# A fused attention and MLP kernel: in-order emission against a list-scheduled program with batch 0 in halves

## The chip, the cores and the metric

One Trainium2 chip (trn2), one core of it. The metric is the device time of one execution in microseconds (us).

Engine names in the profile: PE is TensorE's matmuls, PEld its weight loads, DVE is VectorE, ACT ScalarE, POOL GpSimd, SP the queue from which most transfers are issued.

## The reference

```python
# q, k, v: (4 batches, 4 heads, 1088 tokens, 32) float32; S1, S2: (8, 32)
def phi(x):                                  # 64 features a token and head
    a = einsum('rd,bhsd->bhsr', S1, x)
    b = einsum('rd,bhsd->bhsr', S2, x)
    return einsum('bhsi,bhsj->bhsij', a, b).reshape(*x.shape[:-1], 64)
q_p, k_p = phi(q), phi(k)
kv  = einsum('bhsf,bhsd->bhfd', k_p, v)
z   = sum(k_p, axis=2)
num = einsum('bhsf,bhfd->bhsd', q_p, kv)
den = einsum('bhsf,bhf->bhs', q_p, z)[..., None] + 1e-06
x   = (num / den)                            # tokens x 128: the four heads side by side
h   = x @ w_in                               # 128 -> 2048
g   = maximum(h, 0) + alpha * minimum(h, 0)
out = g @ w_out                              # 2048 -> 128, float32
```

Both kernels rewrite the last part: with W = w_in · diag(alpha) · w_out, the output is x @ W + relu(x @ w_in) @ ((1 - alpha) w_out). So a group of 512 tokens needs 16 hidden products, 16 output products and one product with W, all in bf16. The attention part stays in fp32.

## The kernel before

Keys and queries are loaded in pieces of 32 floats, one transfer for each head:

```python
def load_main(t, src, b):
    for h in range(H):
        nc.sync.dma_start(t[:, :, h], AP(src, offset=(b*H + h)*S*D,
                          ap=[[NJ*D, 128], [D, NJ], [1, D]]))
```

A half batch of queries (512 tokens) is transposed on TensorE, so that the four heads' 32 channels lie on 128 partitions; the features are made for pairs of heads, 64 rows by 128 columns; numerator and denominator for pairs of heads too:

```python
def feat(S_):                        # called for Sa and for Sb
    ps = psum.tile([128, 2, 512], F32, tag="w2")
    for p in range(2):
        nc.tensor.matmul(ps[:, p, :n], S_[64*p:64*(p+1)],      # 64 rows, 128 columns
                         s["qT"][64*p:64*(p+1), :n])
# ... and in nd():
for o in (1, 0):                     # denominator, numerator
    for p in range(2):
        nc.tensor.matmul(ps[64*p:64*(p+1), o], kvz[b][:, p, 64*o:64*(o+1)],
                         s["qp"][:, p])                          # 128 rows, 64 columns
```

The MLP keeps its output features-by-tokens, so each group's output is copied, transposed on TensorE and copied again. The order of work is that of the Python program, in which streams of steps are merged by rough weights:

```python
run(rest_steps(0, "t"))
run(merge(k_steps(0, "t", "h"), setup_steps("h")))      # keys of batch 0, weights
run(merge(k_steps(1, "t"), q_main(0, 0, "h") + q_main(0, 1, "h")))
for b in range(B):                                       # MLP of b beside the keys of b+2
    ...                                                  # and the queries of b+1
    run(merge(m_, ks, qs))
```

## Time and profile before

| | before |
|---|---|
| time, median of 5 | 184.43 us (183.06 to 189.14) |
| span of the profiled run | 179.3 us, granted clock 0.997 |
| first MLP matmul | 55.5 us |
| TensorE busy | 150.5 us, 84% of the span |
| VectorE, ScalarE busy | 83.7, 79.6 us |

The page gives busy times by engine and, in rows of 40 digits, the busy tenths of each slice of the span. The prediction below shows the lines that matter. How to read them: a full row for one engine and half-full rows for the others point to that engine, but "busy" on TensorE is drawn from records that overlap (a record of 0.38 us follows its predecessor by 0.215 us). So the starts of successive records are what a matmul costs.

### The profile page before, as it was taken

How to read it: one execution, taken by the hardware profiler on the slowest of the kernel's cores; microseconds unless marked ns; L12 is line 12 of the kernel's file. 1: busy time of each engine (PE TensorE's matmuls, PEld its weight loads, DVE VectorE, ACT ScalarE, POOL GpSimd, SP SyncE). 2: the span in 40 equal slices, each digit the busy share in tenths (PEclk: the TensorE clock that was granted, in tenths of full speed). 3: DMA queues.
4: the chain of work that ended last, by engine and by line, in shares of the span. 5: the costliest groups of instructions: out<-in, count | busy, mean ns of one | idle time of the engine just before them, and what ended most of it. 6: DMA issues, size and time to landing. Idle time of an engine off the chain costs nothing.

```text
span 179.3 us, 2240 instructions
## 1 busy us (share of the span) xinstructions
PE 150.5 (84%) x817; PEld 82.9 (46%) x828; DVE 83.7 (47%) x152; ACT 79.6 (44%) x149; POOL 17.0 (9%) x35
## 2 busy tenths in 40 slices
PE   0160099999599999999999999999999999999970
PEld 0030099965263545456454554633333434355540
DVE  3010052115623662764558185454656647757740
ACT  2010051051126761755376285535635657657540
POOL 6000499600000000000000000000000000000000
PEclk9999999999999999999999999999999999999998
DMA  2968997599930000010001001000100100101011
GB/s 38 186 115 195 343 228 116 94 220 162 213 56 4 2 0 0 0 62 2 0 0 59 4 0 59 0 0 0 61 1 0 59 0 0 62 0 62 0 59 29
DMA packets 41050, 11.16 MB, mean 62 GB/s; under 512 B 37056, under 2 KB 39376, under 8 KB 40912
## 3 DMA queue, kind: packets, MB, share of 16 engines
q1 hardware_dynamic: 41040, 11.03, 27.4%
q8 instruction: 6, 0.10, 0.3%
q14 instruction: 4, 0.03, 0.1%
HBM read 8.80 MB, written 2.23 MB: 62 GB/s over the span
## 4 chain that ended last, share of the span: by engine, by line
PE 79%; SPq 7%; DMA 5%; ACT 3%; DVE 2%; issue 2%; ACTq 0%
PE ps_h L360 16%; PE ps_o L373 16%; PE ps_kvz L261 10%; PE ps_nd L330 9%; PE ps_ab L235 5%; DMA w_in_f<-in_moe_w_in_dram 5%; SPq L90 3%; PE ps_ot L391 3%; PE ps_qt L300 2%; PE ps_w L212 2%; PE ps_wt L203 2%; PE ps_kt L226 2%; DVE kp L243 1%; PE ps_o L372 1%; SPq L116 1%
## 5 line engine op out<-in xcount | busy, mean ns | idle before, releaser
L364 ACT ACTIVATE rh<-ps_h 128x512 bf16<-128x512 f32 (+1 forms) x98 | 53.5, 582 | 38.5 <-PE ps_h L360 35.9
L360 PE MATMUL ps_h<-xT,w_in_bf 128*128 128x512 bf16 (+1 forms) x139 | 48.6, 367 | 0.6 <-issue 0.2
L373 PE MATMUL ps_o<-rh,w_a_bf 128*128 128x512 bf16 (+1 forms) x138 | 47.3, 366 | 0.2
L366 DVE TENSOR_SCALAR rh<-ps_h 128x512 bf16<-128x512 f32 (+1 forms) x46 | 29.5, 647 | 14.6 <-PE ps_h L360 12.9
L360 PEld LDWEIGHTS <-w_in_bf 128*128 128x128 bf16 x144 | 14.2, 99 | 21.9 <-issue 11.9
L373 PEld LDWEIGHTS <-w_a_bf 128*128 128x128 bf16 x144 | 14.1, 98 | 14.4 <-issue 4.0
L335 DVE STREAM_TRANSPOSE dt<-ps_nd 128x512 f32<-128x512 f32 (+1 forms) x9 | 6.2, 687 | 18.2 <-PE ps_nd L330 18.2
L243 DVE TENSOR_TENSOR kp<-ps_ab,b_sb 128x1024 f32<-128x1024 f32 x8 | 9.8, 1224 | 9.4 <-ACT b_sb L75 9.4
L203 PE MATMUL ps_wt<-ident,w_in_f 128*128 128x128 f32 x16 | 3.9, 397 | 9.5 <-DMA w_in_f<-in_moe_w_in_dram 9.5
L235 PEld LDWEIGHTS ps_ab<-S12blk,kT 128*128 128x128 f32 x68 | 9.5, 211 | 5.1 <-ACT kT L75 2.8
L235 PE MATMUL ps_ab<-S12blk,kT 128*128 128x64 f32 x68 | 10.6, 298 | 1.0 <-ACT kT L75 1.0
L75 ACT COPY kT<-ps_kt 128x512 f32<-128x512 f32 (+1 forms) x9 | 4.7, 522 | 14.7 <-PE ps_kt L226 14.7
L196 POOL TENSOR_SCALAR w_b_f<-w_out_f,S12T_165 128x128 f32<-128x128 f32 x16 | 9.5, 616 | 16.7 <-DMA w_out_f<-in_moe_w_out_dram 16.7
L77 DVE COPY oT<-ps_ot 128x512 f32<-128x512 f32 (+1 forms) x8 | 5.3, 658 | 10.8 <-PE ps_ot L391 10.8
L203 PEld LDWEIGHTS ps_wt<-ident,w_in_f 128*128 128x128 f32 x16 | 3.0, 216 | 10.0 <-DMA w_in_f<-in_moe_w_in_dram 9.9
L75 ACT CAST w_in_bf<-w_in_f 128x512 bf16<-128x512 f32 x3 | 1.7, 615 | 10.7 <-DMA w_in_f<-in_moe_w_in_dram 10.7
L75 ACT COPY qT<-ps_qt 128x512 f32<-128x512 f32 (+1 forms) x9 | 5.2, 573 | 2.7 <-PE ps_qt L300 2.7
L340 DVE STREAM_TRANSPOSE rr<-rc 128x512 f32<-128x512 f32 (+1 forms) x9 | 6.1, 682 | 0.3
L75 ACT COPY b_sb<-ps_ab 128x128 f32<-128x128 f32 (+1 forms) x10 | 2.5, 251 | 7.9 <-PE ps_ab L235 7.9
L391 PE MATMUL ps_ot<-ident,ob 128*128 128x128 f32 x34 | 5.6, 281 | 0.5 <-ACT ob L75 0.5
L261 PE MATMUL ps_kvz<-v_77,kp 128*128 128x96 f32 x32 | 4.3, 282 | 2.0 <-DVE kp L243 2.0
L341 DVE TENSOR_TENSOR xT<-ps_nd,rr 128x512 bf16<-128x512 f32 (+1 forms) x9 | 5.9, 653 | 0.1
(148 smaller groups left out, 170.8 us busy)
## 6 DMA issues: line engine op xcount, KB each, us to landing
out_dram<-oT SPq DMA_DIRECT2D x8, 256.0 KB, 2.0
w_in_f<-in_moe_w_in_dram SPq DMA_DIRECT2D x1, 1024.0 KB, 8.2
k_68<-in_k_dram SPq DMA_DIRECT2D x4, 128.0 KB, 3.0
v_76<-in_v_dram SPq DMA_DIRECT2D x2, 256.0 KB, 3.0
q_72<-in_q_dram SPq DMA_DIRECT2D x4, 128.0 KB, 2.8
k_69<-in_k_dram SPq DMA_DIRECT2D x4, 128.0 KB, 6.6
v_77<-in_v_dram SPq DMA_DIRECT2D x2, 256.0 KB, 3.2
q_73<-in_q_dram SPq DMA_DIRECT2D x4, 128.0 KB, 3.6
```

The costliest lines, as they stand in the source:

```text
L75: nc.scalar.copy(dst, src)
L196: nc.gpsimd.tensor_scalar_mul(w_b_f[:, c], w_out_f[:, c], alphaT[:, c:c + 1])
L203: nc.tensor.transpose(ps[:, c], w_in_f[:, (4 * i + c) * 128:(4 * i + c + 1) * 128], ident)
L235: nc.tensor.matmul(ps[:, j * H:(j + 1) * H], kT[:, j * 128:(j + 1) * 128], S12blk, start=True, stop=True)
L243: nc.vector.tensor_mul(kp[:, :n], bview(av, [list(av.ap[1]), list(av.ap[2]), [0, r]]), bview(bv, [list(bv.ap[1]), [0, r], list(bv.ap[2])]))
L261: nc.tensor.matmul(acc["ps"][:, p], kp_chunk[rows, 2 * p:2 * p + 2].rearrange("s h i j -> s (h i j)"), vt[rows, 3 * p:3 * p + 3], start=fi ...
L330: nc.tensor.matmul(ps[64 * p:64 * (p + 1), o, c0:c0 + nn], kvz_done[b][:, p, 64 * o:64 * (o + 1)], s["qp"][:, p, c0:c0 + nn], start=True, ...
L360: nc.tensor.matmul(ps[:, :n], w_in_bf[:, c * 128:(c + 1) * 128], xT[:, col0:col0 + n], start=True, stop=True)
L364: nc.scalar.activation(rh[:, :n], ps[:, :n], ACTF.Relu)
L366: nc.vector.tensor_scalar_max(rh[:, :n], ps[:, :n], 0.0)
L373: nc.tensor.matmul(s["o"][:, :n], w_a_bf[:, c], s["rh"].pop(c)[:, :n], start=False, stop=c == NC - 1)
L391: nc.tensor.transpose(ps[:, j], s["ob"][:, j * 128:(j + 1) * 128], ident)
```

## The change

The intent: cut TensorE's fp32 work by using more of the array at once, let VectorE do transposes, load in larger pieces, and start the MLP early. The order of all operations is computed by a list scheduler in Python before anything is emitted; it has a cost for every operation, models the buffers, and sorts by due times that a long table of shifts corrects. Batch 0 is worked in token halves, its values loaded in halves around the first queries, its key products given to VectorE or GpSimd, and matmuls on constant tiles fill TensorE's first microseconds.

```diff
+class Op:      # engine(s), cost, dependencies, buffers, due time, emit function
+SHIFT = {"Sab": 13243, "W": 2603, ... some 620 entries ...}
+def plan(ops, classes):   # list scheduling over engines and buffers; returns ops by start
 ...
-    k_sb = [consts.tile([128, NJ, H, D], ...)]
+    k_sb = [consts.tile([128, H, NJ, D], ...)]
+    def main_ap(src, b):                       # all heads in one transfer, 1 KB pieces
+        return AP(src, offset=b*H*S*D, ap=[[NJ*D, 128], [S*D, H], [1, NJ*D]])
+    # batch 0: k in two halves, v half, q half, v half, q half, then the weights
 ...
+    def dummy(n=1):
+        for _ in range(n):
+            nc.tensor.matmul(PS[:, 7], ones(128), ones(512), start=True, stop=True)
+    op("pe", 3750, lambda e: dummy(7), name="warm")
 ...   # queries: VectorE turns 32x32 blocks; features 32 rows x 64 columns, 8 tiles
+        def rnd(i, bufs):
+            def f(e):
+                for t in range(4):
+                    for c in range(2):
+                        nc.tensor.matmul(ps(bufs[t//2])[64*c:64*c+64, t % 2, :nf],
+                                         Sab[32*t:32*t+32, i], moving(sb(bq), t, c))
 ...   # denominator and numerator: 64 rows x 32 columns, 8 tiles
+                for b, h, c, mv, dst in nums(...):
+                    w = kvW[b][s, h] if which else bview(zc[b][s, h:h+1], [[0, D]])
+                    nc.tensor.matmul(dst, w, mv)
 ...   # keys: values as the stationary side, 32 columns, four heads side by side
+                            nc.tensor.matmul(ps(bk)[32*h:32*h+32, :R], v_sb[b][:, h, ...],
+                                             kp[half][...])
 ...   # output: VectorE turns 32x32 blocks from PSUM, no transpose on TensorE
+            op("dve", ..., lambda e: nc.vector.transpose(sb(boT), ps(bo)[:, :n]), ...)
 ...   # last 256 tokens: tokens as the output's partitions, no transpose at all
+    for o in plan(ops, classes):
+        dummy(o.fill)
+        o.emit(o.on)
```

Cuts are marked with dots. Four row groups of tiles need four PSUM banks at a time, so the fixed division of the banks was given up as well: seven are shared and handed out by the schedule.

## The prediction

> **What bounds the kernel now**
>
> I read the page's busy shares and slices first, then TensorE's waits in the steady part, then the busy time of each engine by stage, then TensorE's own order of work, and last the tail.
>
> ```profile
> span 179.3 us, 2240 instructions
> PE 150.5 (84%) x817; PEld 82.9 (46%) x828; DVE 83.7 (47%) x152; ACT 79.6 (44%) x149; POOL 17.0 (9%) x35
> PE   0160099999599999999999999999999999999970
> DMA packets 41050, 11.16 MB, mean 62 GB/s; under 512 B 37056, under 2 KB 39376, under 8 KB 40912
> ```
>
> The first two lines are the page, the third its slices of 4.48 us. TensorE is full from 22 us to the end; VectorE and ScalarE are each under half. The start is bound by loads, cut into packets of under 512 bytes. Between 55 and 165 us TensorE's whole list of waits is two entries:
>
> ```profile
> PE ps_qt L300 <- issue: 0.2, 1, 0.2
> PE ps_h L360 <- issue: 0.2, 1, 0.2
> ```
>
> So no wait can be removed there: only TensorE work can. The stages (columns: stretch, length, busy time and count of PE, PEld, DVE, ACT, POOL, then clock, DMA share, GB/s):
>
> ```profile
> 0.00:13.50 13.50, 3.67 (x12) 2.29 (x12) 2.35 (x21) 2.32 (x4) 2.95 (x18) 1.00 0.60 114
> 13.50:22.00 8.50, 0.00 (x0) 0.00 (x0) 0.35 (x1) 0.00 (x0) 1.81 (x4) 1.00 0.93 272
> 22.00:36.00 14.00, 13.34 (x97) 13.24 (x97) 4.35 (x5) 3.63 (x8) 12.22 (x14) 1.00 0.83 148
> 80.00:110.00 30.00, 29.82 (x166) 16.17 (x168) 15.86 (x26) 16.60 (x31) 0.00 (x0) 1.00 0.03 10
> ```
>
> Eight microseconds pass with TensorE empty, while large weight packets move at 272 GB/s. The first MLP matmul starts only at 55.54 us (the chain of waits). In the order of TensorE's work (start, duration):
>
> ```profile
> 60.42 0.38 PE L360 MATMUL ps_h<-xT,w_in_bf 128*128 128x512 bf16 x1
> 60.64 0.38 PE L373 MATMUL ps_o<-rh,w_a_bf 128*128 128x512 bf16 x1
> 60.85 0.38 PE L360 MATMUL ps_h<-xT,w_in_bf 128*128 128x512 bf16 x1
> 61.21 0.66 PE L235 MATMUL ps_ab<-S12blk,kT 128*128 128x64 f32 x4
> 61.80 1.13 PE L308 MATMUL ps_w_486<-qT,Sa 64*128 64x512 f32 x4
> 67.33 1.92 PE L261 MATMUL ps_kvz<-v_78,kp 128*128 128x96 f32 x16
> 69.18 1.94 PE L330 MATMUL ps_nd<-qp,kz_436 128*64 128x512 f32 x8
> ```
>
> Starts count, not the 0.38 durations: a bf16 matmul of 512 columns costs 0.215 us. Going over to fp32 costs 0.36 - 0.215 = 0.15 more. The fp32 query work costs 1.06 us for one pair of 64-row tiles over 512 columns, and 1.87 for two pairs of 64-column tiles, 0.935 a pair. The tail, from the chain: the last product ends at 173.2, output goes through a copy, a transpose and a copy until 174.54, and four stores end the span at 179.3.
>
> ```profile
> 173.22 0.38 ACT ob L75
> 173.64 0.45 PE ps_ot L391 x2
> 174.12 0.42 DVE oT L77
> ```
>
> **What the Trainium skill says**
>
> "TensorE: Matmul & The Clock Gate", Part 3: matmuls on different 32-row groups run at once, about 4 ns apart, so a set of tiles costs about one matmul. The trace agrees for two 64-row tiles (both inside 1.06 us, where one fp32 matmul of four passes at 0.215 would alone need 0.86); it has no case of eight.
>
> The same page, Part 1: an idle array runs at half rate until some 3.4 us of activity. Agrees in effect: four transposes took 1.12 us at 22.66 and 0.44 at 104.49 us (the chain of waits), although the granted-clock row shows 0.9 and more throughout. The change's constant warm-up matmuls aim here.
>
> "TensorEngine Tiling (Array Packing)", Key Properties: changing the tiling mode drains the array. The 0.15 us above is of that kind, though not isolated.
>
> "DMA: Bandwidth & Descriptors", Specifications: transfers want at least 512 B for line rate. Agrees in direction: 272 GB/s with the weights, 114 before them; issue time is mixed in there.
>
> **The change, part by part**
>
> One batch is 1024 tokens; there are 4.25 batches, 8.5 MLP groups of 512. MLP stays: 33 matmuls x 0.215 = 7.1 us a group, 60.4 in all; the last group by 128-token output pieces adds 0.3: 60.7.
>
> Removed from TensorE: transposes of queries and outputs (2 x 0.6 us a batch each), those of the keys after batch 0 (0.9), half of the query matmul time, and the kvz form. Query features go from 64-row pairs to 32 rows x 64 columns, eight tiles at once, 1024 tokens a round. Before, a batch needs 2 x (1.06 + 1.06 + 1.87) = 8.0 us. After: four rounds (two features, denominator, numerator) of about 0.93 = 3.7. Keys: features two sets of 0.6 = 1.2; the kv product becomes v-stationary with 80 matmul records, which I price at 22 ns from the rest-token denominators of before (32 records of 64 columns between 163.16 and 163.85): 1.8; rest and summary matmuls 0.6; together 3.6, where before it was 0.9 + 1.6 + 4.1 = 6.6.
>
> So a batch with keys: before 14.2 + 8.0 + 1.2 + 6.6 + 1.2 = 31.2 (denominator products are 31.9 us apart for two halves: 69.25, 84.98, 101.22); after 14.2 + 3.7 + 3.6 + about eight switches x 0.15 = 1.2, so 22.7.
>
> TensorE after the first MLP matmul, in sum: MLP 60.7; queries of batches 1 to 3, 11.1; second half of batch 0, 1.9; rest queries 1.3; keys of batches 1 to 3, 10.8; rest keys 0.9; weight product in bf16 (16 transposes, 16 matmuls of 256 columns at 0.11) 2.8; 30 switches 4.5. Sum 94.0.
>
> Start: loads up to the first half of w_in are 2.16 MB; at 272 GB/s that is 7.9 us from about 3.5, so 11.5, and the first half of w_out 13.4. Nine issues of 0.65 us on the queue end well before. The longer chain is the keys: second half lands near 5.6; transpose, copy, features, copy, product, kv, summaries take about 6.5 with cold matmuls; then denominator 0.45, transpose 0.65, add and reciprocal 0.45, transpose 0.65, product 0.6. First MLP matmul: 15 us instead of 55.5.
>
> Start 15, work 94, tail 3.4 (copy 0.3, issue 0.65, 2.3 from last issue to end as before; no transpose) gives 112.4. I add 2 for imperfect waits of in-order engines: span 114.4. Measured minus profiled is 184.4 - 179.3 = 5.1, so 119.5 us.
>
> VectorE and ScalarE, by start distances (VectorE 512 elements 0.60, 1024 elements 1.13; ScalarE 512 in 0.48): a batch gives VectorE query, denominator and reciprocal transposes 3.5, products 2.3, small 0.55, scaling 1.3, output transposes 1.3, keys 2.9: 11.8; ScalarE 2.8; and 32 relus, 26 on ScalarE at 0.48 and 6 on VectorE at 0.61. About 15.4 each, under TensorE's 22.7. GpSimd takes key products: its 2048-element product took 4.52, so four of 512 are 4.5 to 5 us a batch. It does not bound.
>
> **The rivals**
>
> First, PSUM becomes the wait. Query rounds hold up to six of seven shared banks, leaving hidden products one or two where before they had three. For: query products have a long VectorE chain behind them. Against: one bank's relu takes 0.48 to 0.6, and two engines drain. If true, each round costs 0.5 to 1 us more: 17 rounds add 8 to 15 us, 128 to 134.
>
> Second, the first 25 us. VectorE, ScalarE and GpSimd have weight casts, splits into high and low halves, batch 0 and the first relus together; w_out's second half lands near 17. For: GpSimd took 9.5 + 4.5 us for the same weights before. Then group 0 is engine-bound and 4 to 6 us are lost: 124 to 126.
>
> Third, the tiles may not overlap eightfold, or dispatch of twice as many small records may bound. If a round took 1.8 us, 17 rounds add 15: about 134. It would still be much faster.
>
> Fourth, better: switches clustered and rows as fast as four bare passes (0.86). Minus 4 to 6: 114.
>
> **Range and chances**
>
> Even the bad rivals, two at once, leave 135 to 149 against 184.4. I take 119.5, range 113 to 129. Faster by over 2%: 0.98; within 2%: 0.01; slower: 0.01, for something unforeseen such as a static order that stalls.
>
> **What would show it right or wrong**
>
> Right: first MLP matmul at 14 to 17 us; TensorE busy in most slices after; a query round about 0.9 us; a batch about 23 us; under 5 us from last matmul to end. Wrong: relus ending most TensorE idle time (PSUM), TensorE idle between 15 and 27 us (setup), rounds near 1.8 us (no overlap), VectorE over 90% in the steady part, or long "issue" waits on TensorE, which I have no row to price.

## The result, and the profile after

| | before | after |
|---|---|---|
| time, median of 5 | 184.43 us | 114.61 us (114.34 to 115.91) |
| span of the profiled run | 179.3 us | 114.1 us |
| first MLP matmul | 55.5 us | 18.2 us |
| last product | 173.2 us | 110.9 us |
| TensorE busy | 150.5 us (84%) | 105.9 us (93%) |
| VectorE, ScalarE, GpSimd busy | 83.7, 79.6, 17.0 us | 83.1, 75.4, 25.3 us |

The ratio is 0.627, 95% interval 0.622 to 0.633. A ratio is the mean time of one kernel's fast runs over that of the other's of the same rounds, so not quite the ratio of the medians. The five runs of the kernel before, 183.06 to 189.14, were all slower than its fast runs (181.24 to 181.71, below), so the 0.631 measured there is the cleaner figure.

The page of the changed kernel, the lines that answer to the first fence of the prediction:

```profile
span 114.1 us, 3537 instructions
PE 105.9 (93%) x1455; PEld 54.4 (48%) x1455; DVE 83.1 (73%) x157; ACT 75.4 (66%) x163; POOL 25.3 (22%) x25
PE   7987595899999999999999999999999999999980
DMA packets 37536, 11.25 MB, mean 99 GB/s; under 512 B 27008, under 2 KB 37520, under 8 KB 37520
```

TensorE is still the full engine, now from about 20 us of a shorter span. Most packets are still under 512 bytes; there are a quarter fewer of them. TensorE's longest waits (us in total, times, longest; PEq is TensorE's own sequencer):

```profile
PE ps L931 <- DVE aq__76 L861: 1.3, 1, 1.3
PE ps L498 <- PEq L1028: 0.8, 1, 0.8
PE ps L712 <- DVE kpr L652: 0.7, 1, 0.7
PE ps L762 <- DVE zc L741: 0.7, 1, 0.7
```

All four fall before 21 us. By stretches (columns as in the prediction: stretch, length, busy time and count of PE, PEld, DVE, ACT, POOL, clock, DMA share, GB/s):

```profile
10.00:15.00 5.00, 3.44 (x97) 2.18 (x97) 3.60 (x8) 2.83 (x9) 0.76 (x1) 0.87 1.06 294
15.00:20.00 5.00, 3.67 (x66) 1.76 (x51) 3.41 (x7) 2.88 (x8) 5.00 (x6) 0.78 0.98 289
30.00:40.00 10.00, 9.92 (x156) 5.26 (x141) 9.28 (x15) 6.29 (x12) 2.40 (x3) 1.00 0.81 188
60.00:70.00 10.00, 10.00 (x181) 4.98 (x187) 6.30 (x11) 6.52 (x14) 1.95 (x1) 1.00 0.16 28
```

Loads run at 289 to 294 GB/s from 10 to 20 us. The kernel before had 114 up to 13.5 us and then, with the weights, 272 up to 22 us, so the gain lies mostly in its first stretch. The granted clock dips to 0.78 in this run between 15 and 20 us. From 30 to 40 us VectorE is nearly full beside TensorE; from 60 to 70 us it is not.

TensorE's work in order of time:

```profile
43.76 1.09 PE L762 MATMUL ps<-aq__77,zc 64*32 64x512 f32 x16
44.78 1.11 PE L805 MATMUL ps<-qT__75,Sab 32*64 32x512 f32 x16
45.83 0.39 PE L952 MATMUL ps<-rh__83,w_a_bf 128*128 128x512 bf16 x1
46.05 0.38 PE L952 MATMUL ps<-rh__88,w_a_bf 128*128 128x512 bf16 x1
...
57.88 0.23 PE L698 MATMUL ps<-kp__70,v 128*32 128x64 f32 x2
...
58.77 0.20 PE L704 MATMUL ps<-ab__67 128*32 128x32 f32 x2
```

A denominator round for 1024 tokens costs 44.78 - 43.76 = 1.02 us, a feature round 1.05, a bf16 product 0.22. The 64 records of a kv product take 0.89 us, 13.9 ns each. And the end (the chain):

```profile
109.49 1.39 PE ps L949 x22
110.91 0.30 DVE oT__93 L362
111.23 0.27 ACT oT__93 L360
```

The last product ends at 110.9, two copies lead straight to the stores, and the span ends at 114.1: 3.2 us of tail for the 6.1 of before.

Where the 65.2 us between the two spans went, by these marks: the first MLP matmul comes 37.3 us earlier, the stretch from it to the last product is 25.0 us shorter (117.7 to 92.7), the tail 2.9. The first of these is partly a move: ahead of its first MLP matmul the kernel before did the keys of batch 1, all of batch 0's queries and the weight product W. The changed kernel does the keys of batch 1, the rest of the second half of batch 0's queries and most of the weight product later, inside the 92.7.

### The profile page after: what moved, and what is told of

It is laid out like the page before. It is cut to its first block, busy times and chain, and to the rows that moved or that the text cites. A ratio compares the mean times of both kernels' runs of the same rounds, so it can differ in the third digit from the quotient of the medians.

```text
span 114.1 us, 3537 instructions
## 1 busy us (share of the span) xinstructions
PE 105.9 (93%) x1455; PEld 54.4 (48%) x1455; DVE 83.1 (73%) x157; ACT 75.4 (66%) x163; POOL 25.3 (22%) x25
## 4 chain that ended last, share of the span: by engine, by line
PE 80%; DVE 8%; DMA 4%; ACT 3%; SPq 2%; issue 1%; DVEq 0%
PE ps L952 26%; PE ps L931 26%; PE ps L762 9%; PE ps L805 5%; DMA q<-in_q_dram 4%; PE ps L635 3%; PE ps L849 2%; SPq L384 2%; PE ps L949 2%; PE ps L698 2%; PE ps L734 1%; PE ps L588 1%; DVE qT__75 L792 1%; DVE aq__77 L819 1%; DVE aq__76 L861 1%
## 5 line engine op out<-in xcount | busy, mean ns | idle before, releaser
L931 PE MATMUL ps<-xT__96,w_in_bf 128*128 128x512 bf16 (+1 forms) x80 | 22.0, 358 | 1.7 <-DVE aq__76 L861 1.3
L931 PEld LDWEIGHTS <-w_in_bf 128*128 128x128 bf16 x160 | 15.2, 97 | 16.7 <-issue 4.9
L952 PEld LDWEIGHTS <-w_a_bf 128*128 128x128 bf16 x144 | 13.5, 98 | 14.3 <-issue 3.2
L931 PE MATMUL ps<-xT__97,w_in_bf 128*128 128x512 bf16 (+1 forms) x80 | 18.5, 337 | 0.0
L937 ACT ACTIVATE rh__82<-ps 128x512 bf16<-128x512 f32 (+1 forms) x21 | 11.5, 548 | 5.6 <-PE ps L931 5.3
L937 ACT ACTIVATE rh__83<-ps 128x512 bf16<-128x512 f32 (+1 forms) x18 | 9.8, 545 | 4.9 <-PE ps L931 4.5
L652 POOL TENSOR_TENSOR kp__70<-ab__67 128x1024 f32<-128x1024 f32 (+1 forms) x3 | 5.0, 1656 | 28.0 <-ACT ab__67 L360 28.0
L937 ACT ACTIVATE rh__85<-ps 128x512 bf16<-128x512 f32 (+1 forms) x19 | 10.8, 566 | 0.5 <-PE ps L931 0.5
L360 ACT COPY aq__76<-ps 128x1024 f32<-128x1024 f32 (+1 forms) x7 | 5.6, 832 | 7.9 <-PE ps L849 4.5
L937 ACT ACTIVATE rh__86<-ps 128x512 bf16<-128x512 f32 (+1 forms) x16 | 8.9, 558 | 2.2 <-PE ps L952 1.9
L769 DVE STREAM_TRANSPOSE dt__78<-ps 128x1024 f32<-128x1024 f32 (+2 forms) x6 | 5.6, 938 | 4.0 <-PE ps L762 4.0
L937 ACT ACTIVATE rh__84<-ps 128x512 bf16<-128x512 f32 (+1 forms) x15 | 7.8, 519 | 1.0 <-PE ps L931 0.9
L952 PE MATMUL ps<-rh__82,w_a_bf 128*128 128x512 bf16 (+1 forms) x22 | 7.8, 355 | 0.0
L952 PE MATMUL ps<-rh__84,w_a_bf 128*128 128x512 bf16 (+1 forms) x21 | 7.6, 360 | 0.0
L952 PE MATMUL ps<-rh__83,w_a_bf 128*128 128x512 bf16 (+1 forms) x20 | 7.3, 364 | 0.0
L937 ACT ACTIVATE rh__87<-ps 128x512 bf16<-128x512 f32 (+1 forms) x12 | 6.8, 569 | 0.6 <-PE ps L931 0.5
L952 PE MATMUL ps<-rh__85,w_a_bf 128*128 128x512 bf16 (+1 forms) x20 | 7.1, 353 | 0.0
L952 PE MATMUL ps<-rh__86,w_a_bf 128*128 128x512 bf16 (+1 forms) x19 | 6.8, 358 | 0.0
L939 DVE TENSOR_SCALAR rh__84<-ps 128x512 bf16<-128x512 f32 x8 | 5.5, 682 | 1.4 <-PE ps L952 1.1
L959 DVE STREAM_TRANSPOSE oT__91<-ps 128x512 f32<-128x512 f32 (+1 forms) x8 | 5.4, 681 | 1.3 <-PE ps L952 1.1
L778 DVE STREAM_TRANSPOSE rr__80<-dt__78 128x1024 f32<-128x1024 f32 (+2 forms) x6 | 5.6, 932 | 0.2
L952 PE MATMUL ps<-rh__87,w_a_bf 128*128 128x512 bf16 (+1 forms) x16 | 5.7, 354 | 0.0
```

What stands on the lines that cost most here:

```text
L360: nc.scalar.copy(dst, src)
L652: (nc.vector if e == "dve" else nc.gpsimd).tensor_tensor(out=dst, in0=i0, in1=i1, op=ALU.mult)
L769: nc.vector.transpose(bview(sb(dt), [[1, nn]]).rearrange("p (c n) -> p c n", c=2), ps(bd)[:, :, :ncp])
L778: o = op("dve", dv(nn) + 35, lambda e: nc.vector.transpose(sb(rr)[:, :nn], bview(sb(dt)[:, :, 1], [[32, nb], [0, 32]])), [o], [dt, rr], 80 ...
L931: nc.tensor.matmul(ps(b)[:, :n], w_in_bf[:, c * 128:(c + 1) * 128], xs(), start=True, stop=True)
L937: nc.scalar.activation(sb(br)[:, :n], ps(b)[:, :n], ACTF.Relu)
```

## The experiments

All were built on the changed kernel. All gave correct results. Except where it is said, the order computed for the changed kernel was kept and only what is emitted was altered. Runs compared with one another directly ran on one chip; where the chip differs, ratios to the kernel before are compared.

### The changed kernel again (e0_after)

> The changed kernel itself, unaltered, so that small effects of this call are compared on one chip. Expected 114.3 to 115.9 us as before. It also says whether the distance between timed run and span is 1.8 us for the changed kernel, and what it is for the kernel before (the prediction took 5.1 from one profile).

Measured: median 114.41 us; five fast runs with mean 114.44, one slow at 117.88. Ratio to the kernel before 0.631. In every one of these runs the time lay 1.8 us above the span. For the kernel before the fast runs had 181.24 to 181.71 us with spans of 179.3 to 179.7, and the slow ones 183.98 to 184.96 with spans of 181.9 to 183.0 and clocks of 0.972 to 0.978. So the distance is about 1.8 us for the changed kernel and about 2.0 for the kernel before. The 5.1 us of the prediction came from setting a fast profile (span 179.3) beside a median of 184.43, which by its time lies among the slow runs; the clocks of those first runs are not on record.

The profile of this repeat had clock 1.0 throughout, its first MLP matmul at 18.1 us and its span at 112.5. The two equal starts have different causes. In the first profile, the slowest run of its five, the denominator and numerator rounds began at 13.99 us with the clock low, and an add on VectorE after them took 0.37 us; here they began at 13.67, and the same add took 1.06 us; both times it ended when a product on GpSimd beside it did (the last experiment). Over the seven profiles whose start was not meant to change much (both of the changed kernel, by tile, across, rounds twice and both with transposes twice), the first MLP matmul lies between 17.1 and 19.2 us. So a shift of half a microsecond in one profile shows nothing.

### Tiles that follow one another on the same place (e4_quarters_by_tile), and across (e5_quarters_across)

```diff
-                for t in range(4):
-                    for c in range(2):
-                        matmul(bank(t)[64*c:64*c+64, :512], Sab[32*t:32*t+32, i], moving(t, c))
+                for t, c, h in ORDER:        # pieces of 128 columns
+                    matmul(bank(t)[64*c:64*c+64, 128*h:128*h+128],
+                           Sab[32*t:32*t+32, i], moving(t, c)[:, h])
 # by tile:  ORDER = [(t, c, h) for t in range(4) for c in range(2) for h in range(4)]
 # across:   ORDER = [(t, c, h) for h in range(4) for t in range(4) for c in range(2)]
```

> The query feature rounds of batches 1 to 3 (6 rounds of 8 tiles, 512 columns each) are cut into 32 matmuls of 128 columns, issued tile after tile: the four pieces of one tile follow each other. Same arithmetic, same columns. Theory A (the gain of the rounds is overlap of tiles, and starts are in program order): a round, 1.04 us in the changed kernel, becomes about 4 to 6 us, since only the last piece of a tile can overlap the next; TensorE is the bound, so 6 rounds add 18 to 30 us to 114.6: 132 to 145. Theory B (the rounds are fast for another reason, or TensorE is not the bound): 115 to 118.

> The same 32 matmuls of 128 columns per round as in the run by tile, but issued across the eight tiles first, so that neighbours always lie on different tiles. Theory A (overlap): a round stays at 1.0 to 1.2 us and the time within 114 to 117 us. Theory C (the larger number of instructions costs, not the order): as slow as the run by tile.

Measured by tile: median 146.22 us, three of four runs slow; the one fast run 140.04. Across: 116.53 us, fast mean 116.40, ratio 0.640. TensorE's work in order of time, by tile:

```profile
52.84 4.54 PE L805 MATMUL ps<-qT__75,Sab 32*64 32x128 f32 x64
57.31 0.61 PE L958 MATMUL ps<-rh__83,w_a_bf 128*128 128x512 bf16 x1
```

and across:

```profile
52.40 1.21 PE L805 MATMUL ps<-qT__75,Sab 32*64 32x128 f32 x64
53.54 0.39 PE L958 MATMUL ps<-rh__83,w_a_bf 128*128 128x512 bf16 x1
```

The same 64 records cost 4.47 us in one order and 1.14 in the other. This shows that the gain of the small tiles is their overlap, and that the order of issue decides it: a matmul that waits for its own tile holds back all that come after. Theory A holds, C falls. Six rounds at 3.4 us more than the 1.05 of the changed kernel are 20.5 us, so 135; the fast run was at 140. The granted clock in the profiled run, a slow one, fell to 0.67 to 0.87 in stretches with such rounds, which slows what follows (57.31 to 57.71 is 0.40 us for a bf16 product that otherwise takes 0.215). The fast run's own mean clock was 0.963 over a span of 138.3 us; 3.7% of that is 5 us, an estimate from these two numbers, so a lower clock would cover the missing 5 us, but no profile of a fast run shows where. The 2 us that the run across lost are more than six rounds at 0.09; their place is open. Its only profile is of a slow run, and there TensorE once stands idle for 4.3 us in the middle of such a round (up to 38.26 us), with nothing to wait for that the profile shows ("issue"). So a smaller cost of the fourfold number of instructions is not excluded.

### Feature rounds twice (e6_rounds_twice)

```diff
-                for t in range(4):
+                for t in [0, 1, 2, 3] * (2 if nf == 512 else 1):
```

> The query feature rounds of batches 1 to 3 are issued twice, the second over the first: 6 extra rounds of about 1.0 us on TensorE, nothing on other engines. Theory A (TensorE alone sets the pace in the steady part): plus 5.5 to 6.5 us, 120 to 121.5 us. Theory B (VectorE or ScalarE, at 60 to 95 per cent busy by stretch, set the pace and TensorE only looks full because its records are drawn long): plus less than 2 us.

Measured: 119.41 us, four fast runs, 5.0 over the repeat on the same chip (114.44).

```profile
44.36 1.97 PE L805 MATMUL ps<-qT__75,Sab 32*64 32x512 f32 x32
46.26 0.39 PE L952 MATMUL ps<-rh__83,w_a_bf 128*128 128x512 bf16 x1
```

Two rounds in a row take 1.90 us, so the second costs some 0.85: four passes of 512 columns without the way in from bf16. Six of them are 5.1 us, and 5.0 was measured. Time added to TensorE is added to the whole; it is just under the range that was expected because a round in a row is cheaper than a round alone.

### The query transposes of VectorE twice (e7_turn_twice), and only for batches 2 and 3 (e11_turn_twice_late)

```diff
+        def turned(e):
+            for _ in range(2 if nf == 512 else 1):          # the later run: tag in ("q2", "q3")
+                nc.vector.transpose(bview(sb(bq), [[1, n]]), qsrc)
-        o = op("dve", ..., lambda e: nc.vector.transpose(bview(sb(bq), [[1, n]]), qsrc), ...)
+        o = op("dve", ..., turned, ...)
```

> VectorE's transposes of the queries of batches 1 to 3 (1.23 us each) are run twice: 3.4 to 3.7 us of extra VectorE work, none on TensorE. Theory A (TensorE sets the pace): plus 0 to 1 us; the first of them, at 23 us where VectorE is nearly full, may cost its 1.1. Theory B (VectorE sets the pace): plus 3 us or more, 117.5 to 118.5.

> VectorE's query transposes are doubled for batches 2 and 3 only (2.4 to 2.5 us of extra VectorE work); doubling those of batches 1, 2 and 3 cost 3.1 us. Theory A (VectorE shares the pace only until some 40 us, where batch 1 falls; later TensorE alone sets it): plus 0 to 0.5 us, 114.4 to 115. Theory B (VectorE sets the pace throughout): plus 2 us, 116.4.

Measured for all three batches: 117.64 us, four fast runs, 3.2 over the repeat (2.9 by the ratios to the kernel before) for 3.7 us more of VectorE work. That is theory B's number. For batches 2 and 3 alone: one fast run of four, at 116.23, which by its ratio to the fast runs of before (0.639 against 0.631) is 1.5 us over; 2.5 us of work were added. The three slow runs lay at 119.1 to 119.6. My premise for this run was wrong too: I took batch 2's transpose to lie after 40 us, and the order places it at 31.5. Stretches of the repeat of the changed kernel, and then of this run:

```profile
30.00:40.00 10.00, 9.85 (x138) 5.12 (x127) 9.12 (x14) 6.31 (x13) 1.16 (x1) 1.00 0.75 181
50.00:60.00 10.00, 10.00 (x144) 5.14 (x143) 8.06 (x13) 8.30 (x19) 0.59 (x1) 1.00 0.16 28
```

```profile
30.00:40.00 10.00, 8.42 (x102) 4.47 (x92) 9.68 (x15) 5.11 (x12) 0.84 (x1) 1.00 0.80 186
50.00:60.00 10.00, 9.07 (x139) 4.71 (x138) 8.53 (x14) 7.28 (x15) 1.58 (x1) 1.00 0.15 26
```

TensorE loses 1.43 us in the first stretch and 0.93 in the second, the two in which a transpose was doubled. So both of my theories were too simple. TensorE is full, and doubling its work costs the whole of it; yet work added on VectorE also costs most of its length, even in a stretch where VectorE was busy for 81%. The two do not exclude each other: the order is fixed on every engine, the schedule delivers operands just in time, and an idle microsecond on an engine that is full from there to the end is not made up. Why the second stretch has no slack with VectorE at 81%, its trace shows:

```profile
53.95 0.65 DVE L942 TENSOR_SCALAR rh__82<-ps 128x512 bf16<-128x512 f32 x1
54.66 1.02 PE L934 MATMUL ps<-xT__97,w_in_bf 128*128 128x512 bf16 x4 [0.77 <-DVE rh__82 L942]
```

In VectorE's fixed order a relu stands right behind the doubled transpose (it began at 51.85 in the repeat), and the next hidden product waited 0.77 us for it.

### Without the constant matmuls (e2_no_warm), and with more of them (e3_warm_longer)

```diff
 # without:
-        for _ in range(n):
+        for _ in range(0):
             nc.tensor.matmul(PS[:, 7], ones(128), ones(512), ...)
 # more: in the emission loop, for TensorE's operations planned between 12.5 and 20 us
+                o.fill = max(0, int((o.start - was - 250) / DUMMY))
```

> All matmuls on constant tiles are left out (7 at the start, 4 single ones in idle gaps before 12.5 us); everything else in the same order. Theory A (they keep the array at full rate while the loads come, and the start hangs partly on TensorE): transposes, features and first query rounds take up to twice as long, first MLP matmul 1 to 3 us later, 116 to 118 us. Theory B (the start hangs on loads and VectorE alone): plus 0 to 0.5 us.

> Constant matmuls also fill the idle gaps that the schedule foresees between 12.5 and 20 us (some 6 more). In the profile of the changed kernel the granted clock fell to 0.87 and 0.78 between 10 and 20 us, and the denominator and numerator products took 1.96 us for the 0.9 of full rate. Theory A (the fall is for want of TensorE activity and lies on the chain of the start): no fall, first MLP matmul about 1 us earlier where there was one, median 113.3 to 114.5 and the slowest runs gone. Theory B (the clock falls whatever fills the gaps, or constants do not count): no change.

Measured without: median 117.66 us, but four of six runs were slow; the two fast ones have mean 115.90, 1.5 over the repeat, ratio 0.639 against 0.631. That is just under theory A's 116 to 118 and above theory B's 115.5, on two runs. The profile has the denominator product at 14.65 us and the first MLP matmul at 18.69, where the repeat has 13.67 and 18.14; theory A expected 1 to 3 us on the latter, and 0.55 lies inside the spread of other profiles. So it is not settled what the constant matmuls are worth. With more: median 114.70, six fast runs, mean 114.61, no gain over 114.44. No slow run occurred in six, where the repeat had one in six; that is no evidence. In its profile the first MLP matmul came at 17.9, and the next ones waited. So theory A of this run falls as far as time goes.

### The keys of batch 0 in small pieces (e9_k0_as_before)

```diff
     def load_half(name, t, src, b, x):
+        if name == "k":
+            for j in range(4*x, 4*x + 4):                  # 128-byte pieces
+                load(f"{name}{b}.{x}", "sp", t[b][:, :, j],
+                     AP(src, offset=(b*H*S + j)*D, ap=[[NJ*D, 128], [S*D, H], [1, D]]), ...)
+            return
```

> The keys of batch 0 are loaded in the manner of the kernel before: pieces of 128 bytes, eight transfers for the two of the change (there one for each head, here one for each token slot). Theory A (packet size and issues of the first loads set the start): all later loads come 2 to 4 us later, and so does the first MLP matmul: 116.5 to 119 us. Theory B (the start hangs on the chain of engine work): under 1 us.

Measured: median 118.58 us; five fast runs with mean 118.28, 3.8 over the repeat; ratio 0.652. The first MLP matmul came at 22.0 us, 3.9 later. All of the delay reaches the end. Theory A holds. The run was not built to part packet size from the number of issues, which went from two to eight, but its trace leans to the issues: the eight held the SP queue for 4.32 us, where the two of the repeat took 1.00, and the first half of w_in was issued at 8.90 us instead of 5.59. A small load landed a median of 2.3 us after its issue, a large one 3.1, so no loss from the small packets themselves is seen. One stretch of it:

```profile
10.00:15.00 5.00, 5.00 (x132) 3.29 (x132) 2.39 (x6) 0.84 (x2) 1.96 (x2) 0.61 1.01 287
```

TensorE's records, whose ends are modelled and which overlap, fill this stretch, and yet the granted clock is 0.61. They are key and query features, key products and two constant matmuls, after a pause of 1.8 us; which of these lowered the clock no run shows.

### The shift table emptied (e1_no_shift), and batch 0 whole (e10_batch0_whole)

```diff
 # both:
-SHIFT = {"Sab": 13243, ...}
+SHIFT = {}
 # batch 0 whole, besides:
-    KPE = [True, False, False, False]
+    KPE = [False] * 4
-    load_half("k", k_sb, k, 0, 0) ... load_half("v", ...) load_q0(0) ... load_q0(1)
+    load_main("k", k_sb, k, 0); load_rest(...); load_main("q", q_sb, q, 0); load_v(0); ...
-        x[b] = q_main(b, LATE) if b else q_first(LATE)
+        x[b] = q_main(b, LATE)
```

> The table of per-operation shifts of the due times is emptied: the same operations, costs, buffers and list scheduler, but the order that the plain rule gives. Theory A (the change in TensorE work and loads is the gain; the order matters at the edges): 118 to 126 us. Theory B (the tuned order carries the gain): above 135 us.

> Batch 0 is treated as the other batches: keys and queries loaded and worked in one piece of 1024 tokens, keys turned on VectorE, values in quarters as for the other batches; shift table empty, so it stands against the run with the empty table. Theory A (halves let the first MLP matmul start earlier): first MLP matmul 3 to 6 us later than in that run, time plus 2 to 6 us. Theory B (loads and weights set the start anyway): within 1 us of it.

Measured with the empty table: 121.02 us, four fast runs, ratio 0.664. Against 0.631 that is 5% or 6 us; the tuned order is worth that, and theory B, that it carries the gain, falls. Its first MLP matmul came at 18.4 us, hardly later than the 18.1 of the tuned order: what the table gains, it gains after that. Batch 0 whole: 125.99 us, ratio 0.691, so 4% or some 5 us over the run with the empty table, and the first MLP matmul at 24.9 us, 6.5 later. Theory A holds for the time; the start moved slightly more than its 3 to 6 us. Part of the 5 us came with a lower clock: the means of these fast runs are 0.959 to 0.973. The values came in quarters rather than halves there and the keys were turned on VectorE rather than TensorE, so it is the whole treatment of batch 0 that is worth 5 us, not the halves alone.

### GpSimd out of the way of the first denominators (e12_port_free)

```diff
-    for o in plan(ops, classes):
+    order = plan(ops, classes)
+    at = {o.name: o for o in order}
+    order.remove(at["w_a0"])                               # one product of the weights
+    order.insert(order.index(at["w_lo0"]) + 1, at["w_a0"])  # after the next, not before
+    for o in order:
```

The reason was this pair in the repeat of the changed kernel, in order of time:

```profile
15.18 1.04 POOL L555 TENSOR_TENSOR w_a_bf<-w_out_f,omaT 128x512 bf16<-128x512 f32 x1
15.19 1.06 DVE L775 TENSOR_SCALAR dt__78<-dt__78 128x16 f32<-128x16 f32 x1
```

An add of 16 elements a partition lasts as long as the GpSimd product beside it. The Trainium skill, "SBUF — State Buffer", section "SBUF: two separate sides", says that VectorE and GpSimd have one pair of ports in common, an exclusive lock held for a whole instruction, which binds VectorE in some of its operations only. The durations of this pair fit it; that the add is one of these operations is not shown otherwise.

> One GpSimd product of the weights is issued after the next one instead of before it, so that GpSimd is idle when VectorE adds the small constant to the first denominators. In the repeat of the changed kernel that add, of 16 elements a partition, took 1.06 us from 15.19 on and ended with a GpSimd product that ran from 15.18 to 16.22; in two runs where the weights had landed a microsecond earlier it took 0.18 to 0.19. Theory A (VectorE and GpSimd share a port, and the add waits for it on the chain of the start): the add takes under 0.4 us in every profile, first MLP matmul at 17.0 to 17.5 us where it was 18.1, median 113.4 to 114.0, a version slightly faster than the changed kernel. Theory B (the lost time is taken back by the next wait, such as that for the second half of the queries or for the casts of the weights): 114.2 to 114.7.

Measured: median 114.58 us, six fast runs, mean 114.59, ratio 0.631, the same as the changed kernel's 0.631. The order of time in it:

```profile
15.42 0.19 DVE L775 TENSOR_SCALAR dt__78<-dt__78 128x16 f32<-128x16 f32 x1
16.10 1.16 POOL L555 TENSOR_TENSOR w_hl<-w_b_f,w_hl 128x512 bf16<-128x512 f32 x1 [1.16 <-ACT w_hl L360]
...
17.49 0.59 PE L931 MATMUL ps<-xT__96,w_in_bf 128*128 128x512 bf16 x2 [0.89 <-DVE xT__96 L784]
...
18.58 0.59 PE L931 MATMUL ps<-xT__96,w_in_bf 128*128 128x512 bf16 x2 [0.50 <-DVE aq__76 L861]
```

The add took 0.19 us, and the first MLP matmul came 0.65 us earlier. So it is shown that the add waits for the GpSimd product beside it. (In the first profile it ran from 15.95 to 16.32 us, the product beside it until 16.28.) The lock as the reason is the page's. The 0.65 us alone would prove little, since other profiles spread more. Then the third MLP matmul waited for VectorE's product of the second half of the queries (the bracket: idle 0.50 us, released by that product), and the first output product came at 20.03, where the repeat has 19.84. Theory B holds for the time: what was gained at one wait was lost at the next. No version beat the changed kernel.

## Why the prediction was right or wrong

The time lay in the range, 4.9 us below the number of 119.5. By its steps:

- **TensorE bounds, and goes on bounding.** Right. Doubled rounds cost what they take on TensorE (5.0 us measured, 5.1 from the trace).
- **Rounds of about 0.93 us for 1024 tokens.** Nearly right: 1.02 to 1.05 when the round comes after other work, some 0.85 when it follows one of its kind. The third rival, no eightfold overlap, fell; the run by tile shows what it would have cost.
- **Keys.** The kv product was priced at 22 ns a record, 1.8 us; measured 13.9 ns, and 1.1 us with the small products behind it, by starts (57.88 to the next work at 59.01).
- **TensorE's stretch from the first MLP matmul, 94.0 and 2 for waits.** Measured 92.7 with the waits. The sum is right to some 3 us.
- **First MLP matmul at 15 us.** Wrong by 3.2: 18.2, and 18.1 in the repeat. The step that failed is the chain of the start: it counted only work that depends on itself. The denominators, taken to start at 12.1 us (5.6 + 6.5), started at 13.99 in the first profile and 13.67 in the repeat; from there to the first MLP matmul 2.8 us were priced, and 4.2 and 4.5 passed. In the traces VectorE works off queries, keys, rest tokens and weights of batch 0 in one fixed order. In the first profile the chain that ended last begins with the first queries' data, at 8.15 us, and the products then ran at a low clock; in the repeat it begins on TensorE and goes through the keys, and there add and reciprocal took 1.37 us instead of 0.45, because of GpSimd. This is the second rival in part, "the first 25 us"; I had listed it and put nothing of it in the sum.
- **Tail 3.4 us.** Right: 3.2. (The parts listed in the prediction add to 3.25.)
- **5.1 us from span to time.** Wrong: 1.8 for the changed kernel. The other 3 us were, as far as the record shows, the slow state of the kernel before.

The span came out at 114.4 predicted and 114.1 measured, but with a start 3 us too early and waits and work 3 us too long. That these cancel is luck, and so is part of the closeness: the profiled run was the slowest of five, the spans of the others are 112.5 to 113.0. The number for the time then missed mostly because of the last point. The first rival, PSUM, was not seen: the only wait of TensorE on a relu in the first profile is one of 0.2 us; with doubled transposes one of 0.77 appeared.

One reading of the kernel before was half right: its start was put down to packets under 512 bytes. Its chain of waits shows the SP queue issuing transfers one after another, some 0.6 us each, until 14.44 us, and then 8.18 us of waiting for w_in. The run with small key pieces points the same way, to the number of issues.

What I claimed of VectorE, that 15.4 us of 22.7 a batch would leave it off the path, is right on average and wrong as a statement on slack: 3.7 us put on it cost 3.2.

## What to carry to other kernels

Count TensorE by the distance between starts, and count how much of the array each matmul uses: the fp32 query rounds on 64 rows cost 8.0 us a batch before and about 4.1 after (two rounds of 1.05, two of 1.02), and eight small tiles at once only pay when neighbours in the order lie on different tiles. When an engine is full from some point to the end, whatever delays its beginning reaches the end (the small pieces: 3.9 us at the start, 3.8 at the end), whereas removing one wait on a chain of close ones may give nothing. How much of the 25.0 us the moved transposes and the new key product have is not shown: no run takes them back one by one. And before adding an offset between profile and clock time, see that both are of the same state.

## What the Trainium skill lacked or had wrong

- "TensorE: Matmul & The Clock Gate", Part 3, gives the span of a set of tiles, but not what issue order does to it: the same 64 records took 1.14 us across tiles and 4.47 us tile by tile. The page's statement that matmuls stay in program order fits this.
- The same page, Part 1, says that start-to-start never drops below about 25 ns, and names no exception; the 4 ns of its Part 3 are one. Here 64 records on four 32-column tiles started 13.9 ns apart on average: four tiles within some 20 ns, and the next four 56 ns after the first of these began.
- The same page's Part 1 ties the half rate to idle windows. In the run with small key pieces, TensorE's records filled 10 to 15 us and the granted clock was 0.61 on average, after a pause of 1.8 us. The cause is open here.
- "SBUF — State Buffer", SBUF: two separate sides: nothing wrong; the runs add a number, 1.06 us for an add of 16 elements a partition that takes 0.19 with GpSimd idle.
- No page that I read says that a kernel on a single core has a slower state: the kernel before ran at 181.2 to 181.7 us and at 184.0 to 185.0 us on one chip, with mean clocks of 0.996 to 0.997 and 0.972 to 0.978.
